# Fewer first-layer columns for the k1 = 0 slots, and output in blocks of 32 tokens, in a fused Fourier-mixing and hardswish-MLP kernel

## The chip, the cores and the metric

The kernel runs on one core of a Trainium2 chip. The metric is the device time of one execution in microseconds; times below are medians of the fast runs, and a comparison holds only between kernels that ran in the same rounds on the same chip. PE is TensorE, PEld its weight loads, DVE is VectorE, ACT is ScalarE, POOL is GpSimd, SP (SyncE) issues most transfers; SPq and ACTq are the issues of SP's and ACT's queue.

## The reference

```python
X = np.fft.fft(np.fft.fft(x, axis=1), axis=2)      # x: (8, 3008, 256) fp32
y = X.real.reshape(24064, 256)
h = y @ w_in                                        # (256, 2048)
g = h * np.clip(h + 3.0, 0.0, 6.0) / 6.0
out = (g @ w_out).astype(np.float32)                # (2048, 256)
```

## The kernel before

The sequence of 3008 is split as 47 x 64. Output tokens are k = k1 + 47 k2, and because x is real the token of (k1, k2) has a partner at (47 - k1, 63 - k2). So only k1 = 0..23 is transformed, in two matmul stages (stage 1 and stage 2 below); ACT copies the result of stage 2 to `q`, the input of the first layer. The batch goes in four pairs; a pair has 12 chunks of four slots (two k1, both batch elements b), a slot being 64 values of k2. For each slot the first layer gives a part u that is the same in both partners and a part v whose sign differs: u + v belongs to the set, u - v to the partners. A chunk has eight steps `fc`; each step makes u and v two steps ahead (`mlp1`) and multiplies seven combinations into the second layer (`mlp2`): three parts of `a`, and four sums `c` that POOL makes of them. DVE transposes a finished chunk's output in the first steps of the next chunk, and SP sends it. The last chunk (ck = 11) holds k1 = 23 in slots 0 and 1 and k1 = 0 in slots 2 and 3. A slot with k1 = 0 is its own set of partners, so only three of the four slots' worth of columns is kept for the second layer, in either half. (Numbers such as L342 are lines of the kernel whose trace is read.)

```python
# mlp1, cut
u = ps_h.tile([P, 2, KC, N2], F32, tag="uv", name="u")     # PSUM, three buffers for all u and v
v = ps_h.tile([P, 2, KC, N2], F32, tag="uv", name="v")
... matmuls of all 256 columns into u and v ...
... s = qn * WN + u, two instructions of 256 ...           # L331
ns, nm = ch.ns, ch.nm                                      # 3 and 2 slots in the last chunk, else 4
nc.vector.tensor_tensor(u[:, :, 0:ns], s[:, :, 0:ns], v[:, :, 0:ns], op=AL.add)        # L339
relu(t[:, 0, :, 0:ns], u[:, :, 0:ns], 1.0 / 6.0)
if ch.last:
    nc.vector.scalar_tensor_tensor(u[:, :, 3], s[:, :, 3], -1.0, v[:, :, 3],           # L342
                                   op0=AL.mult, op1=AL.subtract)
    relu(t[:, 0, :, 3], u[:, :, 3], -1.0 / 6.0)
nc.vector.tensor_tensor(v[:, :, 0:nm], v[:, :, 0:nm], s[:, :, 0:nm], op=AL.subtract)   # L345
relu(t[:, 1, :, 0:nm], v[:, :, 0:nm], -1.0 / 6.0)
... the gates, a = min(t, 1) * u and a = min(t, 1) * v ...                             # L358
# send, cut: a quarter of the partitions and four blocks at a time
for qd in range(DB):
    queues[i % len(queues)].dma_start(
        out=out_k[ch.pr.p, k1, qd][:, 2 * b:2 * (b + nb)],
        in_=o[qd * DH:(qd + 1) * DH, 2 * sl:2 * (sl + nb)].rearrange("i j h e -> i j (h e)"))
```

## Time and profile before

| what | value | how to read it |
|---|---|---|
| time | 1997.33 us (1996.41 to 1998.31, 3 runs) | the profiled run took 2001.73 us |
| an ordinary step | 4.75 us | start of one u matmul to the next |
| a last chunk with the start of what follows, pair 1 | 44.35 us | ten starts of u, from 1011.28 to 1055.63 |
| end of the last matmul to the end | 7.6 us | the matmuls from 1990.96 run 1.46 us; the span is 2000.0 us |

### The profile page before, as it was taken

Reading aid. Unit: us, or ns where it says so; the run is one execution under the profiler, and the core shown is the slowest. Engines: PE = TensorE matmul, PEld = TensorE weight load, DVE = VectorE, ACT = ScalarE, POOL = GpSimd, SP = SyncE. Lnnn points to the kernel's source line nnn. Section 1 sums busy time; section 2 is a strip of 40 time slices with the busy share of each in tenths; the row PEclk is TensorE's granted clock in tenths of the full one; section 3 lists DMA queues with packets and bytes.
Section 4 is the critical chain, followed back from the end, with each engine's and each line's share of the span. In section 5 each row is a group of like instructions: output and inputs, shape, how many; then the busy total and the mean of one; then the engine's idle time right before and its main releaser. Section 6 shows DMA issues by size and latency. Waiting matters only on the chain.

```text
span 2000.0 us, 28370 instructions
## 1 busy us (share of the span) xinstructions
PE 1967.1 (98%) x9178; PEld 1692.0 (85%) x9178; DVE 1439.4 (72%) x2711; ACT 700.1 (35%) x1196; POOL 1413.5 (71%) x1604
## 2 busy tenths in 40 slices
PE   8899999999999999999999999999999999999998
PEld 5488888888888888888888888888888888888887
DVE  4677767776777676776777776777678777777776
ACT  6533333333333333333333333333333333333323
POOL 3277778786677787777657877778667667666764
PEclk9899999999999999999999999999999999999999
DMA  9502211111112111220111221212110101101000
GB/s 272 167 23 57 57 40 46 49 47 35 27 35 51 41 47 49 53 60 25 38 29 30 58 56 43 59 40 56 35 25 18 31 11 27 27 22 27 21 18 19
DMA packets 158985, 93.54 MB, mean 47 GB/s; under 512 B 131019, under 2 KB 143819, under 8 KB 158838
## 3 DMA queue, kind: packets, MB, share of 16 engines
q1 hardware_dynamic: 148470, 58.03, 12.1%
q0 software_dynamic: 9472, 33.49, 6.1%
q8 instruction: 75, 1.23, 0.3%
q14 instruction: 72, 0.59, 0.1%
q10 hardware_dynamic: 896, 0.20, 0.0%
HBM read 54.32 MB, written 37.33 MB: 46 GB/s over the span
## 4 chain that ended last, share of the span: by engine, by line
PE 92%; DVE 3%; ACT 1%; issue 1%; POOL 0%; DVEq 0%; ACTq 0%; POOLq 0%
PE acc L382 55%; PE v L326 16%; PE u L326 16%; PE ps L226 2%; PE ps L280 2%; DVE a L358 1%; ACT t L355 1%; DVE u L339 1%; DVE s L331 1%; DVE o L440 0%; ACT PM L498 0%; PE wps L563 0%; DVE v L345 0%; PE ps L223 0%; DVE u L342 0%
## 5 line engine op out<-in xcount | busy, mean ns | idle before, releaser
L372 POOL TENSOR_TENSOR c<-a 128x512 f32<-128x512 f32 (+1 forms) x383 | 478.2, 1249 | 451.3 <-PE acc L382 358.0
L382 PE MATMUL acc<-c,G 128*128 128x256 f32 (+1 forms) x3072 | 712.1, 375 | 0.0
L355 ACT ACTIVATE t<-u,half 128x512 f32<-128x512 f32 (+2 forms) x416 | 272.6, 655 | 1104.3 <-DVE u L339 1092.7
L382 PEld LDWEIGHTS acc<-c,G 128*128 128x128 f32 x3072 | 577.5, 190 | 72.7
L331 DVE SCALAR_TENSOR_TENSOR s<-qn,WN,u 128x256 f32<-128x256 f32 x768 | 334.1, 476 | 352.2 <-PE u L326 351.7
L382 PE MATMUL acc<-a,G 128*128 128x256 f32 (+1 forms) x2304 | 550.9, 375 | 0.0
L382 PEld LDWEIGHTS acc<-a,G 128*128 128x128 f32 x2304 | 434.4, 190 | 57.5
L326 PE MATMUL v<-q,W 127*128 127x256 f32 x1536 | 397.7, 381 | 7.6 <-DVE a L358 7.6
L326 PE MATMUL u<-q,W 128*128 128x256 f32 x1536 | 395.4, 380 | 2.0 <-DVE a L358 1.7
L326 PEld LDWEIGHTS u<-q,W 128*128 128x128 f32 x1536 | 287.8, 190 | 59.9 <-issue 15.8
L326 PEld LDWEIGHTS v<-q,W 127*128 127x128 f32 x1536 | 289.7, 190 | 55.5 <-issue 8.1
L358 DVE SCALAR_TENSOR_TENSOR a<-t,u 128x512 f32<-128x512 f32 (+2 forms) x416 | 265.9, 646 | 96.3 <-ACT t L355 90.9
L372 POOL TENSOR_TENSOR c<-c,a 128x256 f32<-128x256 f32 (+1 forms) x383 | 274.5, 717 | 30.0
L372 POOL TENSOR_TENSOR c<-a,c 128x256 f32<-128x256 f32 (+1 forms) x383 | 274.3, 716 | 30.1
L339 DVE TENSOR_TENSOR u<-s,v 128x512 f32<-128x512 f32 (+1 forms) x384 | 263.0, 685 | 41.5 <-DVE s L331 0.9
L355 ACT ACTIVATE t<-v,half 128x512 f32<-128x512 f32 (+1 forms) x384 | 257.2, 670 | 5.8 <-DVE v L345 4.4
L345 DVE TENSOR_TENSOR v<-v,s 128x512 f32<-128x512 f32 (+1 forms) x384 | 257.5, 671 | 1.1
L358 DVE SCALAR_TENSOR_TENSOR a<-t,v 128x512 f32<-128x512 f32 (+1 forms) x416 | 254.8, 619 | 0.5
L372 POOL TENSOR_TENSOR r<-w,e 128x256 f32<-128x256 f32 (+1 forms) x94 | 90.7, 987 | 3.7
L390 ACT ACTIVATE e<-acc 128x512 f32<-128x512 f32 (+2 forms) x190 | 86.3, 545 | 2.8 <-PE acc L382 2.7
L440 DVE STREAM_TRANSPOSE o<-r 128x256 f32<-128x256 f32 (+1 forms) x192 | 72.5, 415 | 0.4
L238 ACT COPY z<-ps 96x512 f32<-96x512 f32 x64 | 37.2, 581 | 83.6 <-PE ps L226 64.0
(90 smaller groups left out, 758.1 us busy)
## 6 DMA issues: line engine op xcount, KB each, us to landing
out_dram<-o SPq DMA_DIRECT2D x732, 32.0 KB
zd<-z SPq DMA_DIRECT2D x32, 384.0 KB
g<-zd SPq DMA_DIRECT2D x48, 256.0 KB
xt<-in_x_dram POOLq DMA_DIRECT2D x21, 384.0 KB, 4.0
qn<-qd SPq DMA_DIRECT2D x23, 256.0 KB
st<-in_moe_w_in_dram POOLq DMA_DIRECT2D x8, 512.0 KB, 11.9
st<-in_moe_w_out_dram POOLq DMA_DIRECT2D x8, 512.0 KB, 5.4
xt<-in_x_dram POOLq DMA_DIRECT2D x7, 376.0 KB, 3.8
```

Of the source, the lines that this page charges most:

```text
L226: nc.tensor.matmul(ps[0:PZ], F[0:PR, 0:PZ], y[:, 2 * i:2 * i + 2, :], start=True, stop=True)
L280: nc.tensor.matmul(ps[:, blk, 2 * u:2 * u + 2], g[:, kk, blk * (P + 1):blk * (P + 1) + P], T[:, :, gr, blk, kk], start=True, stop=True)
L326: nc.tensor.matmul(ps[:, i], W1[r, blk, f * P:(f + 1) * P], q[r, blk, of:of + KC], start=True, stop=True)
L331: nc.vector.scalar_tensor_tensor(s[:, i].rearrange("p k n -> p (k n)"), qn[:, of * N2:(of + KC) * N2], WN[:, f:f + 1], u[:, i].rearrange(" ...
L339: nc.vector.tensor_tensor(u[:, :, 0:ns], s[:, :, 0:ns], v[:, :, 0:ns], op=AL.add)
L345: nc.vector.tensor_tensor(v[:, :, 0:nm], v[:, :, 0:nm], s[:, :, 0:nm], op=AL.subtract)
L355: nc.scalar.activation(t, h, AF.Relu, bias=half[:], scale=scale)
L358: nc.vector.scalar_tensor_tensor(dst, t, 1.0, h, op0=AL.min, op1=AL.mult)
L372: (eng or nc.gpsimd).tensor_tensor(out, in0, in1, op=AL.add)
L382: nc.tensor.matmul(ch.acc[i // 2][:, i % 2, 0:ch.n], G[:, i, fc, :], mv, start=(fc == 0 and i % 2 == 0), stop=(fc == NF - 1), skip_group_c ...
L390: nc.scalar.mul(ch.e[:, k:i + 1, 0:ch.n], ch.acc[i // 2][:, 0:i + 1 - k, 0:ch.n], 1.0 / WS)
L440: nc.vector.transpose(o[:, 0:n // DH, h], ch.r[:, m, h, 0:n].rearrange("p (j i) -> p j i", i=DH))
```

## The change

Its intent: a slot with k1 = 0 needs only k2 = 0..32 multiplied, 194 columns instead of 256 in that chunk; the first half keeps k2 = 0..31 of both batch elements, the second their partners, so that u and v are treated alike. The output blocks of the two halves are then 32 tokens long, and each is sent by itself.

```diff
+    NH = N2 // 2 + 1
-    out_k = out.rearrange("(p bj i k1) (q e) -> p k1 q i bj e", ...)
+    out_k = out.rearrange("(p bj i k1) (q e) -> p k1 bj q i e", ...)
 # stage 2
+            nk = NH if (gr, kk) == (NG - 1, 2 * KK - 1) else N2
+                nc.tensor.matmul(ps[:, blk, u * P:n]..., T[:, :, gr, blk, kk, 0:nk], start=True, stop=True)
 # first layer: nq = P + 2 * NH = 194 in the last chunk, 256 elsewhere
+                nc.tensor.matmul(ps[:, i, 0:nq], W1[...], q[r, blk, of:of + nq], start=True, stop=True)
 # the last chunk
+        nc.vector.tensor_tensor(un, sn, vn, op=AL.add)
+        relu(tn[:, 0], un, 1.0 / 6.0)
+        nc.vector.tensor_tensor(vn, vn, sn, op=AL.subtract)
+        relu(tn[:, 1], vn, -1.0 / 6.0)
+        gate(a[:, 0, :, 0:P], tn[:, 0, :, 0:P], u[:, :, 0:P])
+        for f in range(2):
+            gate(slots(a[:, 0, f], N2 // 2, 1), *(slots(x, NH, 1)[:, :, 0:NH - 1] for x in (t[:, 0, f], u[:, f])))
+        for f in range(2):
+            gate(slots(a[:, 1, f], N2, 0)[:, :, ::-1], ...)
+            gate(slots(a[:, 1, f], N2 // 2, 1)[:, :, ::-1], ...)
 # send
+        for j, (bj, k1) in enumerate(ch.blocks[m]):
+            queues[j % len(queues)].dma_start(out=out_k[ch.pr.p, k1, bj], in_=o[:, j].rearrange("p h e -> p (h e)"))
 ... spread, the loop over slots and the tile shapes follow from these ...
```

More of the change, by code (lines that the diff above doesn't have):

```diff
@@ L82 @@
     TB = KC * N2
+    NH = N2 // 2 + 1
     NG = NCK // 2
-    DB, DH = D // 64, 32
+    DH = 32
     assert S == N1 * N2 and D == 2 * P and B % 2 == 0 and TB == 256 and NK1 % (2 * KK) == 0
@@ L102 @@
     x_pn = x.rearrange("b (n1 n2) d -> (b n1) n2 d", n2=N2)
-    out_k = out.rearrange("(p bj i k1) (q e) -> p k1 q i bj e", p=NP, k1=N1, i=DH, e=2 * DH)
+    out_k = out.rearrange("(p bj i k1) (q e) -> p k1 bj q i e", p=NP, k1=N1, i=DH, e=2 * DH)
     ctx.enter_context(tc.manual_schedule())
@@ L272, in stage2 @@
         if i == 0:
-            pr.q[gr] = qpool.tile([P, 2, 2 * KC, N2], F32, tag="q", name="q")
+            pr.q[gr] = qpool.tile([P, 2, 2 * TB], F32, tag="q", name="q")
         g = pr.g[gr]
-        ps = bank([P, 2, 4, N2], "ps2")
+        ps = bank([P, 2, TB], "ps2")
         for u in range(2):
             kk = 2 * i + u
+            nk = NH if (gr, kk) == (NG - 1, 2 * KK - 1) else N2
+            n = u * P + 2 * nk
             for blk in range(2):
-                nc.tensor.matmul(ps[:, blk, 2 * u:2 * u + 2], g[:, kk, blk * (P + 1):blk * (P + 1) + P],
-                                 T[:, :, gr, blk, kk], start=True, stop=True)
-        nc.scalar.copy(pr.q[gr][:, :, 4 * i:4 * i + 4, :], ps[:])
+                nc.tensor.matmul(ps[:, blk, u * P:n].rearrange("p (b k) -> p b k", b=2),
+                                 g[:, kk, blk * (P + 1):blk * (P + 1) + P],
+                                 T[:, :, gr, blk, kk, 0:nk], start=True, stop=True)
+        nc.scalar.copy(pr.q[gr][:, :, i * TB:i * TB + n], ps[:, :, 0:n])
     def spread(pr, gr):
@@ L293, in spread @@
         else:
+            n = 2 * TB if gr < NG - 1 else 3 * P + 2 * NH
             qd = dpool.tile([1, 2 * TB], F32, tag="qd", name="qd")
-            nc.sync.dma_start(out=qd[:], in_=pr.q[gr][P - 1:P, 1].rearrange("p k n -> p (k n)"))
-            nc.sync.dma_start(out=pr.qn[gr][:], in_=qd[:].to_broadcast([P, 2 * TB]))
+            nc.sync.dma_start(out=qd[:, 0:n], in_=pr.q[gr][P - 1:P, 1, 0:n])
+            nc.sync.dma_start(out=pr.qn[gr][:, 0:n], in_=qd[:, 0:n].to_broadcast([P, n]))
         del pr.g[gr]
@@ L306, in __init__ @@
             self.ns = 3 if self.last else KC
-            self.nm = 2 if self.last else KC
             self.n = self.ns * N2
+            self.nq = P + 2 * NH if self.last else TB
             self.a, self.c, self.acc = {}, {}, {}
             k1 = [(ck * KK + j // 2 + 1) % NK1 for j in range(KC)]
-            rows = [(j % 2, k1[j]) for j in range(KC)], [(j % 2, N1 - k1[j]) for j in range(KC)]
+            self.blocks = [[(2 * (j % 2) + h, (k1[j], N1 - k1[j])[m]) for j in range(KC) for h in range(2)]
+                           for m in range(2)]
             if self.last:
-                rows = rows[0][0:3], rows[1][0:2] + rows[0][3:4]
-            self.rows = rows
+                for m in range(2):
+                    self.blocks[m][4:] = [(m, 0), (2 + m, 0)]
     def mlp1(ch, fc):
-        gr, of = ch.ck // 2, ch.ck % 2 * KC
+        gr, of, nq = ch.ck // 2, ch.ck % 2 * TB, ch.nq
         q, qn = ch.pr.q[gr], ch.pr.qn[gr]
-        u = ps_h.tile([P, 2, KC, N2], F32, tag="uv", name="u")
-        v = ps_h.tile([P, 2, KC, N2], F32, tag="uv", name="v")
+        u = ps_h.tile([P, 2, TB], F32, tag="uv", name="u")
+        v = ps_h.tile([P, 2, TB], F32, tag="uv", name="v")
         for blk, ps in ((0, u), (1, v)):
@@ L325, in mlp1 @@
                 f = fc + i * NF
-                nc.tensor.matmul(ps[:, i], W1[r, blk, f * P:(f + 1) * P], q[r, blk, of:of + KC],
+                nc.tensor.matmul(ps[:, i, 0:nq], W1[r, blk, f * P:(f + 1) * P], q[r, blk, of:of + nq],
                                  start=True, stop=True)
-        s = spool.tile([P, 2, KC, N2], F32, tag="s", name="s")
+        s = spool.tile([P, 2, TB], F32, tag="s", name="s")
         for i in range(2):
             f = fc + i * NF
-            nc.vector.scalar_tensor_tensor(
-                s[:, i].rearrange("p k n -> p (k n)"), qn[:, of * N2:(of + KC) * N2], WN[:, f:f + 1],
-                u[:, i].rearrange("p k n -> p (k n)"), op0=AL.mult, op1=AL.add)
@@ L336, in mlp1 @@
-        ns, nm = ch.ns, ch.nm
-        a = apool.tile([P, 2, 2, KC, N2], F32, tag="a", name="a")
-        t = spool.tile([P, 2, 2, KC, N2], F32, tag="t", name="t")
-        nc.vector.tensor_tensor(u[:, :, 0:ns], s[:, :, 0:ns], v[:, :, 0:ns], op=AL.add)
-        relu(t[:, 0, :, 0:ns], u[:, :, 0:ns], 1.0 / 6.0)
-        if ch.last:
-            nc.vector.scalar_tensor_tensor(u[:, :, 3], s[:, :, 3], -1.0, v[:, :, 3],
-                                           op0=AL.mult, op1=AL.subtract)
-            relu(t[:, 0, :, 3], u[:, :, 3], -1.0 / 6.0)
@@ L345, in mlp1 @@
-        nc.vector.tensor_tensor(v[:, :, 0:nm], v[:, :, 0:nm], s[:, :, 0:nm], op=AL.subtract)
-        relu(t[:, 1, :, 0:nm], v[:, :, 0:nm], -1.0 / 6.0)
-        gate(a[:, 0, :, 0:ns], t[:, 0, :, 0:ns], u[:, :, 0:ns])
-        if ch.last:
-            gate(a[:, 1, :, 2], t[:, 0, :, 3], u[:, :, 3])
-        for i in (slice(0, 2),) if nm == KC else (0, 1):
-            gate(a[:, 1, i, 0:nm, ::-1], t[:, 1, i, 0:nm], v[:, i, 0:nm])
-        ch.a[fc] = a
+            nc.vector.scalar_tensor_tensor(s[:, i, 0:nq], qn[:, of:of + nq], WN[:, f:f + 1], u[:, i, 0:nq],
+                                           op0=AL.mult, op1=AL.add)
@@ new lines, in mlp1 @@
+        a = apool.tile([P, 2, 2, TB], F32, tag="a", name="a")
+        t = spool.tile([P, 2, 2, TB], F32, tag="t", name="t")
+        ch.a[fc] = a
+        if ch.last:
+            activate_last(a, t, s, u, v, nq)
+            return
+        nc.vector.tensor_tensor(u[:], s[:], v[:], op=AL.add)
+        relu(t[:, 0], u[:], 1.0 / 6.0)
+        nc.vector.tensor_tensor(v[:], v[:], s[:], op=AL.subtract)
+        relu(t[:, 1], v[:], -1.0 / 6.0)
+        gate(a[:, 0], t[:, 0], u[:])
+        rev, tk, vk = (m.rearrange("p i (k n) -> p (i k) n", n=N2) for m in (a[:, 1], t[:, 1], v[:]))
@@ new lines, in mlp1, with activate_last, slots @@
+        gate(rev[:, :, ::-1], tk, vk)
+    def activate_last(a, t, s, u, v, nq):
+        un, vn, sn, tn = u[:, :, 0:nq], v[:, :, 0:nq], s[:, :, 0:nq], t[:, :, :, 0:nq]
+        nc.vector.tensor_tensor(un, sn, vn, op=AL.add)
+        relu(tn[:, 0], un, 1.0 / 6.0)
+        nc.vector.tensor_tensor(vn, vn, sn, op=AL.subtract)
+        relu(tn[:, 1], vn, -1.0 / 6.0)
+        def slots(x, n, i):
+            return x[:, i * P:i * P + 2 * n].rearrange("p (b k) -> p b k", b=2)
+        gate(a[:, 0, :, 0:P], tn[:, 0, :, 0:P], u[:, :, 0:P])
+        for f in range(2):
+            gate(slots(a[:, 0, f], N2 // 2, 1), *(slots(x, NH, 1)[:, :, 0:NH - 1] for x in (t[:, 0, f], u[:, f])))
+        for f in range(2):
+            gate(slots(a[:, 1, f], N2, 0)[:, :, ::-1], *(slots(x, N2, 0) for x in (t[:, 1, f], v[:, f])))
+            gate(slots(a[:, 1, f], N2 // 2, 1)[:, :, ::-1], *(slots(x, NH, 1)[:, :, 1:NH] for x in (t[:, 1, f], v[:, f])))
@@ L360, in combine @@
     def combine(ch, fc):
-        a = ch.a[fc][:].rearrange("p m f k n -> p (m f) (k n)")[:, :, 0:ch.n]
+        a = ch.a[fc][:].rearrange("p m f n -> p (m f) n")[:, :, 0:ch.n]
         c = cpool.tile([P, 4, TB], F32, tag="c", name="c")
@@ L374, in mlp2 @@
     def mlp2(ch, fc):
-        a = ch.a.pop(fc)[:].rearrange("p m f k n -> p (m f) (k n)")[:, :, 0:ch.n]
+        a = ch.a.pop(fc)[:].rearrange("p m f n -> p (m f) n")[:, :, 0:ch.n]
         c = ch.c.pop(fc)
@@ L444, in send @@
         queues = [nc.sync, nc.scalar] if ch.final else [nc.sync]
-        i = 0
-        sl = 0
-        while sl < ch.ns:
-            b, k1 = ch.rows[m][sl]
-            nb = 2 if sl + 1 < ch.ns and ch.rows[m][sl + 1] == (b + 1, k1) else 1
-            for qd in range(DB):
-                queues[i % len(queues)].dma_start(
-                    out=out_k[ch.pr.p, k1, qd][:, 2 * b:2 * (b + nb)],
-                    in_=o[qd * DH:(qd + 1) * DH, 2 * sl:2 * (sl + nb)].rearrange("i j h e -> i j (h e)"),
-                )
-                i += 1
-            sl += nb
+        for j, (bj, k1) in enumerate(ch.blocks[m]):
+            queues[j % len(queues)].dma_start(out=out_k[ch.pr.p, k1, bj], in_=o[:, j].rearrange("p h e -> p (h e)"))
     pairs = [Pair(p) for p in range(NP)]
```

## The prediction

> **What bounds the kernel now.** I read the page first: the busy row, then the chain that ended last.
>
> ```profile
> PE 1967.1 (98%) x9178; PEld 1692.0 (85%) x9178; DVE 1439.4 (72%) x2711; ACT 700.1 (35%) x1196; POOL 1413.5 (71%) x1604
> ...
> PE 92%; DVE 3%; ACT 1%; issue 1%; POOL 0%; DVEq 0%; ACTq 0%; POOLq 0%
> ```
>
> TensorE is the bound nearly everywhere. The kernel makes 4 pairs x 12 chunks x 8 steps; one step multiplies four blocks of the first layer (u and v, 256 columns each) two steps ahead and seven blocks of the second. The change shortens only the first layer of the twelfth, last chunk of each pair, whose second layer already has 192 columns. So I looked at that chunk alone: start times of the u matmuls in the timeline give its steps, and the busy time in those windows says who is full. Pair 1, from the step that starts the second u of the chunk (columns: window and length, then PE, PEld, DVE, ACT, POOL busy):
>
> ```profile
> 1016.92:1021.68 4.76, 4.76 (x24) 4.19 (x23) 2.80 (x7) 2.12 (x5) 2.18 (x3) 1.00 0.16 56
> 1021.68:1025.69 4.01, 4.01 (x24) 3.80 (x23) 2.61 (x8) 2.58 (x6) 3.20 (x5) 1.00 0.00 0
> 1025.69:1029.91 4.22, 4.22 (x23) 3.71 (x23) 3.28 (x10) 1.42 (x3) 4.06 (x5) 1.00 0.00 0
> 1029.91:1034.03 4.12, 4.12 (x25) 3.72 (x24) 3.31 (x10) 1.06 (x2) 3.80 (x6) 1.00 0.08 18
> 1034.03:1038.71 4.68, 4.24 (x24) 3.71 (x23) 3.83 (x12) 1.42 (x3) 2.19 (x3) 1.00 0.28 65
> 1038.71:1043.39 4.68, 4.24 (x23) 3.71 (x23) 3.75 (x11) 1.79 (x4) 2.18 (x3) 1.00 0.16 37
> 1043.39:1047.51 4.12, 4.12 (x25) 3.72 (x23) 3.23 (x9) 1.42 (x3) 2.18 (x3) 1.00 0.00 0
> 1047.51:1051.63 4.12, 4.12 (x23) 3.71 (x23) 3.44 (x9) 1.49 (x3) 2.18 (x3) 1.00 0.01 2
> 1051.63:1055.63 4.00, 4.00 (x24) 3.79 (x23) 3.60 (x7) 1.43 (x3) 2.62 (x3) 1.00 0.00 0
> ```
>
> An ordinary step is 4.75 us for 22 MATMULs of 256 columns (each product is two of them): 0.2159 us each. A step with 192 columns in its second layer needs 8 x 0.2159 + 14 x 0.1625 = 4.00 us, which the second and last rows show. The rows of 4.12 and 4.68 are therefore not TensorE's own. DVE in one of them:
>
> ```profile
> 1040.35 0.86 DVE L331 SCALAR_TENSOR_TENSOR s<-qn,WN,u 128x256 f32<-128x256 f32 x2
> 1041.32 0.56 DVE L339 TENSOR_TENSOR u<-s,v 128x384 f32<-128x384 f32 x1
> 1042.59 0.30 DVE L342 SCALAR_TENSOR_TENSOR u<-s,v 128x128 f32<-128x128 f32 x1 [0.71 <-ACT t L355]
> 1042.92 0.43 DVE L345 TENSOR_TENSOR v<-v,s 128x256 f32<-128x256 f32 x1
> 1043.39 0.75 DVE L358 SCALAR_TENSOR_TENSOR a<-t,u 128x384 f32<-128x384 f32 x2
> 1044.07 0.48 DVE L358 SCALAR_TENSOR_TENSOR a<-t,v 128x128 f32<-128x128 f32 x2
> ```
>
> The next s is at 1044.46, so the row of DVE work takes 4.11 us: one chain, with a 0.71 us wait inside it, because L342 writes the u tile while ACT still reads it. In the 4.68 steps two output transposes are added, and TensorE shows the wait:
>
> ```profile
> 1035.49 1.10 PE L326 MATMUL v<-q,W 127*128 127x256 f32 x4 [0.44 <-DVE a L358]
> ```
>
> v of one step takes the PSUM buffer of u of the step before (three buffers, two used per step), which the gate has to have read.
>
> **What the Trainium skill says.** "TensorE: Matmul & The Clock Gate", section "Wait — 56ns, not 53.3ns?", gives a warm matmul N / 2.4 GHz + about 2.5 ns start to start. The trace agrees if fp32 takes two cycles per column in each MATMUL: 512 / 2.4 + 2.5 = 215.8 ns against 215.9. It gives 162.5 ns for 192 columns and 164.2 for 194. The same page, "LDWEIGHTS (loading the stationary operand)", makes a weight load columns / 1.2 GHz, 107 ns for 128, whatever is multiplied. The eight stage-2 matmuls of 128 columns stand 0.89 us / 8 = 111 ns apart, so nothing here contradicts it, and it would hold a 66-column matmul near 107. "VectorE: DVE Perf Modes", section "The TRN2 errata — SBUF-src ops pay a fixed extra latency per instruction", has (N + 151) / 0.96 ns for an fp32 tensor_tensor: 557 ns at 384 against 562 measured, 424 at 256 against 432. But start to start they overlap: 0.60 us for 512 elements, 0.20 for 128, thus N / 0.96 + 0.07, and I use that for what DVE costs.
>
> **The change, part by part.**
> 1. First layer of the last chunk, 256 to 194 columns: 8 x (0.2159 - 0.1642) = 0.41 us less TensorE time per step. A step with both short layers becomes 8 x 0.1642 + 14 x 0.1625 = 3.59 us.
> 2. DVE in that chunk. Removed: L342 and its 0.71 us wait, since u and v are now each one sum over all 194 columns. Added: three gates, seven narrower ones where there were four (9 instructions become 11). In order: s pair to sum u, 0.97 - 2 x 62 / 960 = 0.85; sum u to relu 0.65, relu over 388 elements 0.59 (between 0.58 for 384 and 0.69 for 512), to the gate 0.05; gates of u 256, 64, 64 elements: 0.34 + 0.14 + 0.14; gates of v 128, 64, 128, 64: 0.20 + 0.14 + 0.20 + 0.14. Sum 3.42 us. The sum of v lies in the wait for the relu. So the DVE chain (3.42) drops below TensorE (3.59), and the bound is TensorE again, with 0.17 us to spare per step.
> 3. The transposes: 0.69 us in each of two successive steps. Relative to a u start, s is at 0.81 + 0.04, sum u at 1.70, the last gate of u ends at 3.67; v of the next step wants that buffer at 3.59 + 0.65 = 4.24, so DVE may lag about 0.52 us (with 0.05 for the signal) before TensorE waits. First transpose step: lag 0.69 - 0.17 = 0.52, just hidden. Second: 1.04, of which 0.52 appears. So about 0.5 us of wait per pair instead of 0.44 + 0.45 beside the slow chain.
> 4. Sum per chunk, pair 1 (u of step 0 at 1011.28 to 1055.63, 44.35 us): first step, which also has a stage-2 half, 5.64 - 0.41 = 5.23; 4.76 - 0.41 = 4.35; 6 x 3.59 = 21.53; the two steps that already start the next pair's 256 columns, 4.00 each; 0.5 wait: 39.6. Saved 4.75. Pair 2 has the same starts. Pair 0 took 45.00 (its timeline has a relu 0.3 us late at 554.25 and a gate that waited 0.4 at 546.51): 5.2 saved, as such accidents may remain. Pair 3 up to its second layer's step 6, 1952.37 to 1987.71, 35.34: 2 x 4.34 + 21.53 + 0.5 = 30.7, saved 4.6. Together 19.3 us.
> 5. Stage 2 of k1 = 0: two products of 66 instead of 128 columns per pair, four MATMULs; at most 4 x 52 ns x 4 pairs = 0.8 us, and nearly nothing if weight loads hold them. I count 0.1.
> 6. Output: 8 sends per half stay 8, but take all partitions for one block of 32 tokens, with the same 128 pieces of 256 bytes; in the last chunk 8 become 6. DMA is hidden (in the list of waits the longest of an engine for the output is 1.7 us, once), except at the end, where SP and ACT issued 8 each in 3.64 and 3.76 us, and the span ends 2.4 us after. Three instead of four per queue after the last transpose: about 0.5 us off.
> Total 19.3 + 0.1 + 0.5 = 19.9 us: 1997.33 - 19.9 = 1977.4.
>
> **Rivals.**
> A. *Only the matmul columns count*: 32 steps x 0.41 = 13.2 us, 1984. For it: the page says TensorE at 98%. Against: the rows of 4.12 and 4.68 are longer than the matmuls in them, and L342's wait goes too.
> B. *DVE takes over.* It has 11 instructions where it had 9 per step, and slack is only 0.17. If the small gates cost 0.20 instead of 0.14 each, the chain is 3.66: then 6 x 0.07 and the whole of the transposes, 1.38 less 0.5, make about 0.8 us more per pair, 1981. If they cost 0.3, 1984. For it: no 64-element gate is in the trace. Against: a 6-element sum occupies DVE 0.08 us at 53.00 in its timeline.
> C. *POOL in step 1*, where combining the finished chunk (4.2 us) is added to 2.2 us: rows of 4.06 and 3.80 busy. In the trace of pair 1 POOL ends that extra work at 1029.4, has the first c at 1030.4, and TensorE wants it at 1032.6. After the change TensorE is 1.9 us earlier there (0.41 + 0.41 + 0.42 + 0.63 from four steps, 1030.7 with 0.4 less of first layer in the step itself: 1030.3), and POOL is fed about 1.4 us earlier (1029.0). It still holds, with 1.3 us instead of 2.2; a miss costs under 1 us per pair: 1980.
> D. *The new send pattern disturbs the queue* (longer issue, delayed spread or g loads). A chunk lasts 38 us and its 16 issues some 9 us, so even doubled it is hidden, save at the end: up to 2 us.
>
> **Range and chances.** All hidden perfectly with stage 2 gained: 1974.5. B and C together: 1983. Repeats of the kernel before span 2 us. Range 1973 to 1983.5. A gain over 2% needs 40 us, twice what the stage holds; a loss would need the sends to stall everything.
>
> **What would show it.** Steps of 3.6 us in the last chunk where 4.12 stood; no DVE wait like L342's; one PE wait of v of about 0.5 us per pair in place of two of 0.44; DVE's row near 3.4 us plus whatever it idles for u; 12 sends per last chunk. Wrong if those steps stay near 4 us, if gates of 64 elements cost 0.2 or more start to start, if TensorE waits for c of POOL, or if ordinary chunks no longer run at 4.75.

## The result, and the profile after

The changed kernel took 1979.61 us (1978.68 to 1981.95, 4 runs) against 1996.87 us (1995.42 to 1998.31, 4 runs) of the kernel before: 17.3 us less. The ratio is 0.9915, with a 95% interval of 0.9898 to 0.9932: faster, but by less than 2%. (A ratio here is the mean time of one kernel's fast runs over that of the other's of the same rounds, so not quite the ratio of the medians that are quoted.) The predicted value was 1977.4 and the range 1973 to 1983.5.

The busy row and the chain of waits of the changed kernel, from its page:

```profile
PE 1949.1 (99%) x9178; PEld 1685.4 (85%) x9178; DVE 1433.5 (72%) x2775; ACT 687.9 (35%) x1164; POOL 1414.2 (71%) x1604
...
PE 93%; DVE 2%; ACT 1%; issue 0%; DMA 0%; SPq 0%; DVEq 0%; ACTq 0%
```

They say only that TensorE is still the bound. The last chunk of pair 1 says where the time went. Busy time by step in the changed kernel, from the same step as in the prediction (window, its length, then PE, PEld, DVE, ACT and POOL busy):

```profile
1006.84:1011.18 4.34, 4.34 (x25) 3.98 (x23) 3.06 (x11) 2.56 (x6) 1.50 (x3) 1.00 0.16 56
1011.18:1014.77 3.59, 3.59 (x23) 3.59 (x22) 2.37 (x8) 1.89 (x5) 3.23 (x5) 1.00 0.02 6
1014.77:1018.37 3.60, 3.60 (x25) 3.60 (x24) 3.13 (x13) 1.06 (x2) 3.44 (x4) 1.00 0.00 0
1018.37:1021.96 3.59, 3.59 (x24) 3.59 (x23) 3.24 (x13) 0.71 (x2) 3.35 (x6) 1.00 0.06 13
1021.96:1025.70 3.74, 3.74 (x23) 3.56 (x23) 3.59 (x13) 0.77 (x2) 3.25 (x5) 1.00 0.26 58
1025.70:1029.73 4.03, 3.83 (x24) 3.56 (x23) 3.42 (x13) 1.70 (x4) 2.18 (x3) 1.00 0.27 60
1029.73:1033.32 3.59, 3.59 (x24) 3.59 (x23) 3.17 (x14) 1.06 (x2) 2.18 (x3) 1.00 0.06 12
1033.32:1037.33 4.01, 4.01 (x24) 3.80 (x23) 3.01 (x11) 1.17 (x2) 2.19 (x3) 1.00 0.00 0
1037.33:1041.34 4.01, 4.01 (x25) 3.76 (x23) 3.62 (x7) 1.19 (x3) 2.45 (x3) 1.00 0.01 2
```

Where 4.12 stood there is now 3.59, TensorE's own need for 8 matmuls of 194 and 14 of 192 columns. DVE's row of work in the step that ends the chain, in order of time:

```profile
1027.15 0.73 DVE L339 SCALAR_TENSOR_TENSOR s<-qn,WN,u 128x194 f32<-128x194 f32 x2
1027.99 0.57 DVE L360 TENSOR_TENSOR u<-s,v 128x388 f32<-128x388 f32 x1
1028.46 0.56 DVE L362 TENSOR_TENSOR v<-v,s 128x388 f32<-128x388 f32 x1
1029.34 0.68 DVE L379 SCALAR_TENSOR_TENSOR a<-t,u 128x256 f32<-128x256 f32 x3 [0.32 <-ACT t L376]
1029.94 0.74 DVE L379 SCALAR_TENSOR_TENSOR a<-t,v 128x128 f32<-128x128 f32 x4
```

The next s starts at 1030.60, so the chain is 3.45 us long (3.42 was reckoned). The write that had to wait 0.71 us for ACT is gone; the sum of v lies where the relu of u runs, and only 0.32 us of that relu is left to wait for. Seven gates instead of four cost little: the four of v, with 128, 64, 128 and 64 elements, take 0.66 us from start to start. TensorE's one labelled wait in this chunk:

```profile
1026.72 0.90 PE L334 MATMUL v<-q,W 127*128 127x194 f32 x4 [0.20 <-DVE a L379]
```

Against the kernel before, start of u to start of u over the same ten intervals, the chunk takes 39.73 us instead of 44.35 in pair 1; the four chunks together give 4.77 + 4.62 + 4.62 + 4.51 = 18.5 us.

Two more places moved. The step with stage 2 of the narrow slot became 0.15 to 0.16 us shorter in three of four pairs. The stage-1 matmul after it, first in the kernel before and then in the changed one (pair 1), waits less for ACT's copy:

```profile
936.84 1.10 PE L226 MATMUL ps<-y,F 94*96 94x512 f32 x2 [0.68 <-ACT q L282]
...
927.17 1.10 PE L227 MATMUL ps<-y,F 94*96 94x512 f32 x2 [0.57 <-ACT q L287]
```

And the end became longer. The timeline of the end in the kernel before (start, duration, what): the last matmuls, and the sends that ACT's queue issues.

```profile
1990.96 1.46 PE L382 MATMUL acc<-c,G 128*128 128x192 f32 x8
...
1993.86 3.76 ACTq L451 DMA_DIRECT2D out_dram<-o  x8
```

The same in the changed kernel, whose span is 1978.3 us:

```profile
1967.36 1.46 PE L403 MATMUL acc<-c,G 128*128 128x192 f32 x8
...
1970.27 4.88 ACTq L467 DMA_DIRECT2D out_dram<-o  x6
```

Both begin to send 1.44 us after the last matmul. But ACT's six sends take 4.88 us to issue where its eight took 3.76 (SP's: 3.78 and 3.64), and the end comes 3.2 us after the last one was issued instead of 2.4. From the last matmul to the end are 9.5 us instead of 7.6. The time of a single issue (lowest, median and highest, in ns; the kernel before, then the changed one) shows that one of the six took 1.38 us, by the trace the first:

```profile
L451 ACTq DMA_DIRECT2D out_dram<-o x8: 384/440/443, 1993.9 to 1997.2; - x8
...
L467 ACTq DMA_DIRECT2D out_dram<-o x6: 552/674/1380, 1970.3 to 1974.5; - x6
```

So 18.5 + 0.5 - 1.9 = 17.1 us are accounted for, and 17.3 measured. That the two agree to 0.2 us is partly luck, since the start of the program scatters by more (see after_again). The spans of the two traces differ by more, 21.7 us, because the profiled run of the kernel before (2001.73 us, above all its timed runs) was late from the start: its first u started at 84.21 us, that of the changed kernel at 80.06, long before anything that was changed had run.

### The profile page after: what moved, and what is told of

The parts are those of the page before. It is cut to its first block, busy times and chain, and to the rows that moved or that the text cites. A ratio compares the mean times of both kernels' runs of the same rounds, so it can differ in the third digit from the quotient of the medians.

```text
span 1978.3 us, 27746 instructions
## 1 busy us (share of the span) xinstructions
PE 1949.1 (99%) x9178; PEld 1685.4 (85%) x9178; DVE 1433.5 (72%) x2775; ACT 687.9 (35%) x1164; POOL 1414.2 (71%) x1604
## 4 chain that ended last, share of the span: by engine, by line
PE 93%; DVE 2%; ACT 1%; issue 0%; DMA 0%; SPq 0%; DVEq 0%; ACTq 0%
PE acc L403 56%; PE v L334 16%; PE u L334 16%; PE ps L284 2%; PE ps L227 2%; DVE a L379 1%; DVE s L339 1%; ACT t L376 0%; ACT PM L509 0%; DVE o L461 0%; PE wps L574 0%; DVE u L360 0%; PE ps L224 0%; PE ex L514 0%; PE awake L597 0%
## 5 line engine op out<-in xcount | busy, mean ns | idle before, releaser
L376 ACT ACTIVATE t<-u,half 128x512 f32<-128x512 f32 (+1 forms) x384 | 261.0, 680 | 1100.5 <-DVE u L349 1018.7
L339 DVE SCALAR_TENSOR_TENSOR s<-qn,WN,u 128x256 f32<-128x256 f32 (+1 forms) x768 | 330.0, 471 | 354.3 <-PE u L334 354.0
L334 PE MATMUL v<-q,W 127*128 127x256 f32 (+1 forms) x1536 | 390.1, 376 | 4.4 <-DVE a L379 4.4
L334 PE MATMUL u<-q,W 128*128 128x256 f32 (+1 forms) x1536 | 388.3, 375 | 2.4 <-DVE a L379 2.1
L349 DVE TENSOR_TENSOR u<-s,v 128x512 f32<-128x512 f32 x352 | 245.0, 696 | 37.7 <-PE v L334 0.8
L379 DVE SCALAR_TENSOR_TENSOR a<-t,v 128x512 f32<-128x512 f32 (+1 forms) x480 | 263.2, 564 | 0.0
L351 DVE TENSOR_TENSOR v<-v,s 128x512 f32<-128x512 f32 x352 | 243.7, 692 | 0.0
```

The lines of the kernel that those rows point to most:

```text
L334: nc.tensor.matmul(ps[:, i, 0:nq], W1[r, blk, f * P:(f + 1) * P], q[r, blk, of:of + nq], start=True, stop=True)
L339: nc.vector.scalar_tensor_tensor(s[:, i, 0:nq], qn[:, of:of + nq], WN[:, f:f + 1], u[:, i, 0:nq], op0=AL.mult, op1=AL.add)
L349: nc.vector.tensor_tensor(u[:], s[:], v[:], op=AL.add)
L351: nc.vector.tensor_tensor(v[:], v[:], s[:], op=AL.subtract)
L376: nc.scalar.activation(t, h, AF.Relu, bias=half[:], scale=scale)
L379: nc.vector.scalar_tensor_tensor(dst, t, 1.0, h, op0=AL.min, op1=AL.mult)
```

## The experiments

Two submissions of four kernels each; the kernel before ran beside them (1998.12 us in nine runs, and 1998.07 in ten, of which nine are the runs listed for the first submission; so the second is compared in the main with earlier rounds). All eight gave correct results. The reading is the time from the start of one u matmul to the next, which after the first three steps of the program repeats to 0.02 us between runs in which nothing at that step was changed. In pair 1 (pair 2 is within 0.14 us of it; the tenth interval, not shown, is 4.00 or 4.01, and 4.08 in transposes_spread):

```
step (us)                 0    1    2    3    4    5    6    7   next  sum of ten
kernel before          5.64 4.76 4.01 4.22 4.12 4.68 4.68 4.12  4.12       44.35
sends_only             5.64 4.76 4.00 4.23 4.11 4.69 4.68 4.12  4.11       44.35
changed kernel         5.23 4.34 3.59 3.60 3.59 3.74 4.03 3.59  4.01       39.73
old_sends              5.23 4.35 3.59 3.59 3.60 3.74 4.02 3.60  4.00       39.73
full_columns           5.65 4.75 4.01 4.01 4.00 4.05 4.40 4.01  4.00       42.89
wait_back              5.23 4.34 3.60 3.89 4.26 4.91 4.90 4.26  4.46       43.86
gates_six              5.23 4.34 3.59 3.60 3.59 3.62 3.96 3.59  4.00       39.53
transposes_spread      5.23 4.34 3.59 3.60 3.59 3.59 3.60 3.71  4.00       39.33
best                   5.23 4.34 3.60 3.59 3.59 3.59 3.60 3.59  4.01       39.15
```

### sends_only: the kernel before with the new sends

```diff
-            for qd in range(DB): ... o[qd * DH:(qd + 1) * DH, 2 * sl:2 * (sl + nb)] ...
+            for h in range(2):
+                queues[i % len(queues)].dma_start(out=out_b[ch.pr.p, k1, 2 * b + h],
+                                                  in_=o[:, 2 * sl + h].rearrange("p h e -> p (h e)"))
```

> The kernel before, with only its output sent in blocks of 32 tokens (6 sends per half in the last chunk, all 128 partitions as source). Theory: such a send takes longer to issue (a median of 536 ns on the SP queue and 674 ns on the ACT queue in the changed kernel, against 430 and 440 before); this is hidden everywhere but at the end, so the stretch from the end of the last matmul to the end grows from 7.6 to about 9.5 us and the time by about 1.9 us, to 1998.8; steps of the last chunk stay at 4.00 to 4.68 us. Rival 1 (my prediction): fewer sends shorten the end by 0.5 us, 1996.4. Rival 2: the new sends delay something in the middle as well, so the time grows by clearly more than the end does.

Measured: 2002.09 us, 4.0 above the kernel before; ratio 1.002, interval 1.0007 to 1.0034. The end in its timeline (the span is 2000.3 us):

```profile
1989.42 1.46 PE L384 MATMUL acc<-c,G 128*128 128x192 f32 x8
...
1992.32 4.86 ACTq L451 DMA_DIRECT2D out_dram<-o  x6
```

From the last matmul to the end are 9.4 us, and issuing takes 4.86: the new form of send makes the end 1.8 us longer by itself. No step of u after the third of the program moved by more than 0.02 us, so nothing was delayed in between and Rival 2 falls. Rival 1, my prediction for the end, falls too. The time was 3.3 us above the 1998.8 expected, and the other 2 us of its growth are not shown by a trace: the first three steps took 17.28 us here and 15.75 in the trace of the kernel before, but the first u of that trace came 3 us later, in a run of 2001.73 us. They end before the first send, so the likely cause is the scatter of the start that after_again shows below.

### old_sends: the changed kernel with the sends of before

```diff
-        for j, (bj, k1) in enumerate(ch.blocks[m]): ...
+        for j0 in range(0, len(ch.blocks[m]), 4):
+            group = ch.blocks[m][j0:j0 + 4]
+            k1, bj = group[0][1], slice(0, 4) if len(group) == 4 else slice(m, 4, 2)
+            for qd in range(D // 64):
+                queues[i % len(queues)].dma_start(out=out_q[ch.pr.p, k1, qd][:, bj],
+                    in_=o[qd * DH:(qd + 1) * DH, j0:j0 + len(group)].rearrange("i j h e -> i j (h e)"))
+                i += 1
```

> The changed kernel with the sends of before (a quarter of the partitions, four blocks each; 8 per half in the last chunk too). Theory: the end goes back from 9.5 to about 7.6 us, the rest stays, so 1979.6 - 1.9 = 1977.7, and the step times of the last chunk are those of the changed kernel (3.59, 4.03). Rival: the end is longer for another reason (fewer transfers per queue, or chance), and the time stays at 1979.6.

Measured: 1977.91 us, ratio 0.9898 (0.9882 to 0.9913). The last matmuls end at 1967.77 + 1.46 and the span is 1976.8 us: 7.6 us, as in the kernel before, with eight sends issued in 3.75 us. All steps are those of the changed kernel. Together with sends_only this shows that the send's form costs the 1.9 us. What in the form costs it, the 128 source partitions or the shape of the destination, was not taken apart. The pages hold a hint that was not used, the packets of ACT's queue in the kernel before and in the changed one:

```profile
q10 hardware_dynamic: 896, 0.20, 0.0%
...
q10 hardware_dynamic: 792, 0.20, 0.0%
```

Both move the same 768 pieces of 256 bytes. The rest are packets of 4 bytes, 16 for each old send (128 / 8) and 4 for each new one (24 / 6). By the traces at most 18 packets of this queue were under way at once at the end before and at most 7 after, and the last piece landed 0.7 us after the last issue before and 1.9 us after it in the changed kernel. So the new sends seem to run on fewer DMA engines; no run tests this.

### wait_back: the changed kernel with the sum of u in two pieces

```diff
-        nc.vector.tensor_tensor(un, sn, vn, op=AL.add)
-        relu(tn[:, 0], un, 1.0 / 6.0)
+        for c in (slice(0, 3 * N2), slice(3 * N2, nq)):
+            nc.vector.tensor_tensor(u[:, :, c], s[:, :, c], v[:, :, c], op=AL.add)
+            relu(t[:, 0, :, c], u[:, :, c], 1.0 / 6.0)
```

> The changed kernel with 194 columns, but the sum of u made in two pieces, 192 columns and 2, each followed by its relu, so that the second write of u waits again for ACT reading it, as L342 did. Theory: the DVE chain is the bound of this chunk, and goes from 3.42 to about 4.1 (0.85 for s; 1.28 to the second piece; about 0.6 to 1.3 until the gates; 1.3 for the gates), so the steps are 4.0 to 4.2 us and not 3.59, about 3.2 us more per pair, 13 us in all: 1992. Rival A (the columns of TensorE are what counts, DVE lies beside it): the steps stay near 3.6, at most 1981.

Measured: 1999.78 us where 1992 was expected; ratio to the kernel before 1.0008 (0.9992 to 1.0023). With all the narrower matmuls in place, nothing is left of the gain. Two lines of DVE's timeline and the busy row of a step (PE, PEld, DVE, ACT, POOL):

```profile
1038.45 0.56 DVE L361 TENSOR_TENSOR u<-s,v 128x384 f32<-128x384 f32 x1
1039.72 0.17 DVE L361 TENSOR_TENSOR u<-s,v 128x4 f32<-128x4 f32 x1 [0.71 <-ACT t L377]
```

```profile
1039.97:1044.23 4.26, 3.83 (x25) 3.56 (x23) 3.28 (x13) 1.43 (x4) 2.19 (x4) 1.00 0.01 2
```

A sum of four elements, 0.17 us of work, waits 0.71 us for ACT, and the step is 4.26 us long with TensorE busy for 3.83. That is a little more than the 4.0 to 4.2 expected. Steps of the four chunks sum to 15.8 us more than in the changed kernel (13 expected); in the traces the start adds 3.3 us to that (first u at 83.36 us instead of 80.06). So the narrower columns, with this chain, are worth only 18.5 - 15.8 = 2.7 us: in pair 1 steps 0 to 3 gain 1.6 us against the kernel before, and the later ones lose 1.1. That loss shows that the edit puts back a little more than the wait of L342: the seven gates stay, a second relu of u (0.27 us) comes in, and the chain is 4.25 us long (s at 1037.62, the next at 1041.87), where it was 4.11. The narrower columns with the chain exactly as it was were not run; the three steps that gain with any chain would give about 4 x 1.24 = 5 us (an estimate from steps 0 to 2 of the table). Either way most of the gain is lost, and Rival A falls.

### full_columns: the changed kernel with all columns multiplied

```diff
-    NH = N2 // 2 + 1
+    NH = N2
-... slots(x, NH, 1)[:, :, 0:NH - 1] ... slots(x, NH, 1)[:, :, 1:NH] ...
+... slots(x, NH, 1)[:, :, 0:N2 // 2] ... slots(x, NH, 1)[:, :, 1:N2 // 2 + 1] ...
```

> The changed kernel with all 256 columns multiplied again (33 becomes 64 in stage 2, first layer and sums), but its own order of sums and gates kept, without the wait of L342. Theory: TensorE needs 4.00 us per step, DVE about 3.87 (0.98 + 1.59 + 1.30), so steps are 4.00 instead of 4.12 and 4.22, with about 0.6 us of wait after the transposes: about 43.0 us per chunk where 44.35 stood, 1.4 to 2 us per pair, 6 in all; with the longer sends at the end (1.9) that makes 1996.9 - 6 + 1.9 = 1993. Rival A: without fewer columns nothing is gained, 1997 to 1999. Rival C: the wait was all of it, and the time is near 1984.

Measured: 1996.14 us (ratio 0.9984, 0.9968 to 0.9999), 3 us above what was expected. The steps are as expected, though:

```profile
1027.15:1031.15 4.00, 4.00 (x23) 3.79 (x23) 3.69 (x13) 0.82 (x3) 3.69 (x6) 1.00 0.07 16
...
1039.60:1043.61 4.01, 4.01 (x25) 3.80 (x24) 3.62 (x13) 1.45 (x3) 2.18 (x3) 1.00 0.00 0
```

TensorE is full for the whole of the step, at the 4.00 us that 256 columns need. The chunks give 1.67, 1.46 and 1.47 us in pairs 0 to 2 and 1.25 in the seven steps of pair 3: about 6 us, as expected. The end is 9.4 us, as with any of these sends. That leaves 6 - 1.9 = 4 us; the times show 2. The difference is within the scatter of the start, but no trace shows that it is that. Not run was the smallest test of the wait: the kernel before with L345, the sum of v, moved in front of L342, so that the wait is filled and nothing else changes.

### after_again: the changed kernel once more

> The changed kernel itself, once more, on the chip and in the rounds of the next three. All theories: about 17 us under the kernel before; the steps of its last chunks as in its first trace (3.59; 3.74 and 4.03 after the transposes). What it adds: whether the first u of the program starts near 80 us again or near 83, as in other builds.

Measured: 1983.57 us (1979.76 to 1989.0, 6 runs; ratio 0.9926, 0.9911 to 0.994), 14.5 us below the kernel before. This is the same program as in the first submission. Its steps in the last chunks differ from the first trace by 0.01 us at most, and the end is 9.4 us. But its first u starts at 84.38 us where the first trace has 80.06, and its first three steps took 17.12 us instead of 15.36. So the first 95 us of the program differ by up to 6 us between executions of one kernel, and no difference of 2 or 3 us between medians here means anything by itself. What decides it was not studied. The median of this second submission, 1983.57, lies 6.2 us above the predicted 1977.4, so the 2.2 us of the first one owe something to luck; the steps, which repeat, are the better test of the prediction.

### gates_six: one gate fewer

```diff
-        gate(a[:, 0, :, 0:P], ...)
-        for f in range(2):
-            gate(slots(a[:, 0, f], N2 // 2, 1), ...)
+        gate(a[:, 0, :, 0:P + h], t[:, 0, :, 0:P + h], u[:, :, 0:P + h])
+        gate(a[:, 0, :, P + h:P + 2 * h], t[:, 0, :, P + NH:P + NH + h], u[:, :, P + NH:P + NH + h])
```

> The changed kernel with the gates of u as two instructions (160 columns, then 32) where it has three: one DVE instruction less per step. Theory: DVE costs N / 0.96 + 0.07 us per instruction start to start, so the chain falls by 0.07 us per step; the wait after the transposes is what is left of it, 0.15 + 0.44 us per pair, and falls by about 0.14 to 0.2: 0.4 to 0.45 per pair, under 1 us in all. Rival: DVE is not what those two steps wait for, and they stay at 3.74 and 4.03.

Measured: 1980.75 us (ratio 0.9911, 0.9896 to 0.9926), which cannot tell it from the changed kernel by its time. The steps do: 3.62 and 3.96 us after the transposes instead of 3.74 and 4.03, so 0.19 to 0.20 per pair in pairs 1 to 3 and 0.41 in pair 0. The wait answers to DVE's length, in the size expected; the rival falls.

### transposes_spread: one transpose per step

```diff
-        if prev and fc < 3:
+        if prev and fc < 5:        # finish at 0, then one of four transposes in each step
 ... store makes one transpose per call, and sends after every second one ...
```

> The changed kernel with one output transpose in each of steps 1 to 4 of the following chunk instead of two in each of steps 1 and 2. Theory: each adds 0.35 us to a DVE chain that has 0.14 to 0.25 us to spare per step, so DVE falls behind by 0.1 to 0.2 us per step, 0.4 to 0.8 in four, and only what exceeds about 0.5 becomes a wait: 0 to 0.3 us per pair in place of 0.59, so 1 to 2.4 us in all. Rival: the wait is due to something else of the transposes (their wait for the output's transfer), and just moves or doubles.

Measured: 1981.29 us (ratio 0.9915, 0.99 to 0.993), no difference in time that stands out. In pair 1 the steps after the transposes fall from 3.74 and 4.03 to 3.59 and 3.60, and 0.12 us comes back one step later (pair 0 keeps 3.95 and 3.78): 0.4 to 0.6 us per pair, 1.9 us in the trace from the first u to the last. The rival falls: spreading shrinks the wait.

### best: the sends of before, six gates, spread transposes

> All three: the sends of before, gates of u in two, transposes spread. Theory: no wait after the transposes (2.4 us in all), the end as in the kernel before (1.9 us): 4.3 us below the changed kernel, apart from where its start falls (79 to 83 us to the first u). Rival: something in the order of the sends and the spread takes it back, and it stands at the 1977.9 of the old sends alone.

Measured: 1977.38 us (1975.66 to 1980.81), ratio to the kernel before 0.99 (0.9884 to 0.9915); the changed kernel in the same rounds took 1983.57. This version beats both. By the traces it is 2.6 us shorter than the changed kernel from the first u to the last, and the end is 7.5 us instead of 9.5, so 4.5 us (4.3 expected), of the 6.2 between the medians; the rest is not shown, and is within the scatter of the start. By time alone it cannot be told from the 1977.91 of old_sends, which was the rival; the steps tell them apart. Its steps are TensorE's own 3.59 to 3.61 but for one of 3.72 in pair 0 and one of 4.14 for 4.01 after pair 2.

## Why the prediction was right or wrong

**What bounds the kernel, and the wait of L342: right, and shown.** That the 4.12 us steps were DVE's chain and not TensorE's columns was the step on which the rest stood. wait_back puts the wait back, with a second relu, and loses 15.8 of 18.5 us.

**Part 1, the columns: right.** 0.41 us per step, 3.59 for a step with both layers short: measured 0.41 to 0.42 and 3.59 to 3.60. With the wait put back they are worth 2.7 us (about 5 with the chain as it was, by the estimate above), because a step is as long as the longer of TensorE's work and DVE's chain.

**Part 2, DVE's chain: right.** 3.42 reckoned (its terms as printed add up to 3.44), 3.45 measured. Alone, with all columns kept, it is worth 6 us. The two parts give 9 to 11 us taken singly and 18.5 together: each lowers one of two limits that stood at 4.12 and 4.00.

**Part 3, the transposes: right in kind, a little small.** About 0.5 us of wait per pair was predicted, in one step. It was 0.15 + 0.44 = 0.59, since the first transposes were not just hidden. gates_six and transposes_spread show that both follow DVE's length and the bunching of the transposes.

**Part 4, the sum: 19.3 predicted, 18.5 measured.** Half of the difference is pair 0 (5.2 against 4.77), where I had let half a microsecond of accidents vanish; its two steps after the transposes are 3.90 and 4.31, longer than elsewhere. The rest is 0.1 per pair of the longer wait.

**Part 5, stage 2: 0.1 predicted, 0.5 measured, by another way.** The narrow matmuls themselves hardly shorten the group of eight (1.05 to 1.00 us): in the trace all but one of their starts are still 112 ns apart, as if the weight loads held them, as the prediction had allowed. But ACT's copy of the result became shorter, from 0.59 to 0.48 us, and the next stage-1 matmul, which waits for that PSUM buffer, waits 0.57 instead of 0.68. That I had not looked at.

**Part 6, the end: wrong in sign.** The step that failed is "Three instead of four per queue after the last transpose: about 0.5 us off". It took a send to cost the same to issue whatever its form. On ACT's queue six sends of the new form took 4.88 us to issue and eight of the old 3.76, and the end became 1.9 us longer; sends_only and old_sends show it both ways. Rival D named this possibility with the right size, and I did not count it in. This term is 2.4 us off (+1.9 instead of -0.5), the largest of the miss: with 0.8 from part 4 and -0.4 from part 5 the traces put the prediction 2.8 us too low, the medians 2.2.

**The rivals.** A (only columns count, 1984) came near the measured time by its number, but its mechanism fell in two runs. B (small gates cost more) fell: four gates in 0.66 us. (Its own figures were also added wrongly: 6 x 0.07 and 1.38 - 0.5 make 1.3 us per pair, not 0.8.) C (POOL) fell: TensorE has no wait for POOL's c in that chunk, though POOL is busy for 3.44 us of 3.60. D held at the end and, by the steps, nowhere else.

## What to carry to other kernels

When a stage has two limits close together, such as a full engine and a chain through other engines, reckon each alone and take the longer one per step: trimming either by itself gives little, and both together can give more than the two single gains. Look for a second write to a tile that another engine is still reading, even of a few elements; making one write of two can be worth more than the work that the change was meant to save. And price a transfer's issue by its form before changing it, above all at the end of a program, where the issue stands in line with nothing beside it.

## What the Trainium skill lacked or had wrong

- "DMA: Bandwidth & Descriptors", section "Issuing engines are not separate DMA queues", calls the sequencer time of a DMA "usually small relative to the DMA itself". For one send that agrees (0.44 us to issue, and 2.4 us from the last issue to the end). It says nothing of several sends in a row on one queue, whose issues add up: at the end of this program 3.76 us for eight, and 4.88 for six of the other form.
- I found no page with what the issue of one send costs by its form: in 256-byte pieces, ACT's queue needed a median of 0.44 us for a send from 32 partitions (eight sends, 32 KB or 16 KB, with no difference) and 0.67 us for one of 32 KB from 128 partitions (six sends, the first of them 1.38 us). How a send's form sets the number of its DMA engines is in the pages.
- "VectorE: DVE Perf Modes", section "The TRN2 errata — SBUF-src ops pay a fixed extra latency per instruction", gives the length of a single operation, (N + 151) / 0.96 ns, and the trace agrees: 561 ns by it at 388 elements, 567 and 563 measured for the two sums. It must not be summed over a run of operations: gates of 128, 64, 128 and 64 elements took 0.66 us from start to start, where the formula gives 1.03 us (an estimate from that page: 2 x 290 + 2 x 224 ns). The skill has the cost of a run too, in another place than this section.
- Nothing wrong was found in "TensorE: Matmul & The Clock Gate", section "Wait — 56ns, not 53.3ns?": at a new width, 194 columns of fp32 counted as 388 cycles, it gives 164.2 ns, and the step that this makes, 3.59 us, is the one measured.
